# A fused attention and two MLPs on one core: the opening spread over nine slots, with five of the eight weight pairs prepared in it

## The chip, the cores and the metric

The kernel runs on one core of a Trainium2 chip. A core has a matrix engine (TensorE, PE in the rows), a vector engine (VectorE, DVE), a scalar engine (ScalarE, ACT), a general engine (GpSimd, POOL), and a sync engine (SP) whose work here is to issue transfers. Each engine takes its instructions in the order in which they were written for it; between engines semaphores decide. The metric is device time in microseconds of one execution, median over runs.

## The reference, cut to what matters

```
scores = q_c @ k_c^T / sqrt(64)          # 8 x 8 heads, 576 tokens, in chunks of 64
attn   = exp(scores - max) / (sum + 1e-9)
x      = attn @ v_c                      # -> 4608 tokens x 512
h      = relu(x @ w_in) ** 2 @ w_out     # 512 -> 2048 -> 512
out    = (silu(h @ w_gate) * (h @ w_val)) @ w_out2    # 512 -> 1536 -> 512
```

All inputs are float32 or come as float64 words (the weights), which the kernel decodes on the chip. Outputs are float32.

## The kernel before, in words

The 4608 tokens are nine blocks of 512. A block is worked as a "set": set 0 is block 0 alone, sets 1 to 4 are two blocks each, so that seven products of half size stand for eight (the class `Pair`; a single block uses `Single`). The program goes through four stages: `x @ w_in` for all sets (`up1`), then `w_out`, then gate and value, then the last product. The change touches only the first stage, and of that the part up to the end of set 1.

**Attention** comes in units of 256 tokens, two to a block. One unit's chain is: load q and k (`attn_qk`, L324); 64 small matmuls into the PSUM tile `s` (`attn_products`, L335); maximum and difference on DVE (`attn_less_max`: `mx`, `e`); exp on ACT; sum and reciprocal on DVE and a multiply on POOL (`attn_normed`, L368, into `e`); a transposition; 64 matmuls with v into `xps` (`attn_values`); four copies to `x` on ACT (`attn_out`, L450). Units 0 to 5 (`EARLY`: sets 0 and 1) are transposed on PE (`attn_turn_pe`, `et`, L392). Units of later sets are transposed by DVE into `z`, copied on ACT into `p` (L418), and then four transfers of 64 KB on SP's queue exchange quarters (`p<-z`, L422). The tiles `s` of any unit and `xps` of a later unit come from a pool with one buffer (`psa`), so they exclude each other.

**Weights** are prepared in pairs of f tiles; there are eight pairs, `("i", 0)` to `("i", 7)`. `prep_pair` (L192) is a generator of seven steps: take two raw tiles; decode on ACT (four instructions, L129 and L130); clamp and shift on DVE (L134, L135) with two adds on POOL (L139); two `m<-raw,m` instructions on DVE (L144) and two casts on ACT; the low parts and four sums on DVE (L157, L213 to L216); one cast on ACT; the last low part on DVE, and a store of the finished weights `W` (1.8 MB) for the pairs that are loaded again later. `wp` has five buffers for such `W`; pairs 0, 3 and 6 stay in three of them, the others pass through the other two.

**Products.** `up1.run(n, m)` makes the products of set n with weight pair m. A product of half size is six matmuls of 128x512. For a pair of blocks the order is px, pz, then the two late products of the run before (`p4`, `p3`) between which px is continued (`p6`), then py and px again (`p27`). Before px is continued ACT copies it away (`r1`, `u2`, `u3`, L535). For the single block a run is 24 matmuls into two `py` tiles, evicted by ACT (L603, L613), and the two late products are empty. All tiles of 4 KB per partition (q, k, v, e, z, p, raws, x, hi, lo, g) share one pool of 31 buffers (`big`); a tile waits until the last reader of its buffer is done, and for a `g` that is its store.

**The order before.** In the opening (L756) the order on PE, ACT, DVE and POOL is the written one. Slot i holds unit i's products up to its normalisation, unit i-1's transposition, unit i-2's product with v, and seven steps of preparation, three of pair i and three of pair i-1 plus one load; so eight pairs take the opening. From slot 4 on `up1.run(0, m)` follow, three in slot 4 and one in each slot after it. When the loop is over seven of the eight runs of set 0 are done, and the eighth stands behind `up1.run(1, 0)`. In the part after the opening only PE's order is the written one; the other engines' was set by a scheduler. There a run of a pair of blocks is cut into four quarters, and `WHEN` (L985) says at which quarter t of the 32 each step of the next set's four units is placed: loads at -3, 2, 6, 10, products at 2, 6, 10, 14, transposition at 6, 10, 14, 18, product with v at 11, 15, 19, 23. `OPS` (L986) places the splitting of the next set's seven operands into high and low parts.

Of the kernel before, what the change touches and what calls it, by code (L numbers as in the profile page):

```python
# [28 lines left out]
def attention_mlp_mlp_kernel(  # L29
# [29 lines left out]
    nc = tc.nc  # L59
# [9 lines left out]
    upb = BLOCK // UNIT  # L69
# [122 lines left out]
    def prep_pair(key, raws, keep, store):  # L192

        pair = raws.take(2)
        yield
        m = duo("m")
        decode1(pair, m)
        yield
        decode2(pair, m)
        yield  # L200
        decode3(pair, m)
        w = new_combo()
        a1, a22 = m[:, 0, :].rearrange("p (i c) -> p i c", i=2), m[:, 1, half:]
# [12 lines left out]
        tt(out=s4, in0=a12, in1=s2, op=ALU.subtract)  # L216
        yield
        high(s, w[:, 0, 3:7, :])
        yield
        low(s, w[:, 0, 3:7, :], w[:, 1, 3:7, :])  # L220
        if store:
            wdram[key] = combo_dram(key)
            nc.sync.dma_start(out=wdram[key], in_=flat(w))
        if keep:
            combos[key] = w
        yield
# [103 lines left out]
    def attn_v(u):  # L330
        vt = duo("v")
        loader(u).dma_start(out=vt, in_=v[2 * u:2 * u + 2].rearrange("n p c -> p n c"))
        vs[u] = vt
# [326 lines left out]
    work = Work()  # L660
# [8 lines left out]
    def raws_of(keys, ahead):  # L669
        return Raws([sources[name][2 * fp + t] for name, fp in keys for t in range(2)], ahead)  # L670
# [56 lines left out]
            self.late()  # L727


    make_identity(nc, ident)  # L730
    raws1 = raws_of(keys1, 0)
    preps = [prep_pair(key, raws1, True, key in moving1) for key in keys1]
    up1 = Products(keys1, moving1, 2, 1, lambda key: squared)

    def x_sums(n):
        up1.ops[n] = Operands()
# [1 line left out]

    early = list(range(EARLY))
    ready = {"x": upb + 2, "pair": len(early) + 2}

    def prepare(f, steps=1):
        if 0 <= f < n1:
            for _ in range(steps):
                next(preps[f])

    def loads(i):
        if i < len(early):  # L750
            attn_qk(early[i])
        prepare(i)
        if 1 <= i <= len(early):
            attn_v(early[i - 1])

    with ordered(ET.PE, ET.Activation, ET.DVE, ET.Pool):  # L756
        make_identity(nc, ident)
        loads(0)
        loads(1)
        given = 0  # L760
        for i in range(n1 + 1):
            loads(i + 2)
            unit = early[i] if i < len(early) else None
            turned = early[i - 1] if 0 <= i - 1 < len(early) else None
            valued1 = early[i - 2] if 0 <= i - 2 < len(early) else None
            if unit is not None:
                attn_products(unit)
            if turned is not None:
                attn_turn_pe(turned)
            if valued1 is not None:  # L770
                attn_values(valued1)
            prepare(i)
            prepare(i - 1)
            if i == ready["x"]:
                x_sums(0)
                up1.ops[0].make(1, 2, 4)
            prepare(i - 1)
            if i == ready["pair"]:
                x_sums(1)
                up1.ops[1].make(1, 5)  # L780
            if turned is not None:
                attn_turned(turned)
            prepare(i)
            if unit is not None:
                attn_less_max(unit)
                attn_exp(unit)
            prepare(i - 1)
            if i == ready["pair"]:
                up1.ops[1].make(6, 2, 7)
            if unit is not None:  # L790
                attn_normed(unit)
            if valued1 is not None:
                attn_out(valued1)
            if i >= ready["x"]:
                while given < min(n1, i - 1):
                    up1.run(0, given)
                    given += 1
            prepare(i)

    class Down:  # L800

# [181 lines left out]

    LAST = 4 * n1
    WHEN = {"qk": (-3, 2, 6, 10), "scores": (2, 6, 10, 14), "turn": (6, 10, 14, 18), "out": (11, 15, 19, 23)}  # L985
    OPS = {-6: (1, 5), -4: (6,), -3: (2, 7), -1: (4,)}  # L986

    def attention_step(n, t):

        if n < len(sets):  # L990
            units = [b * upb + x for b in sets[n] for x in range(upb)]
            for what in ("out", "turn", "scores", "qk"):
                for u, when in zip(units, WHEN[what]):
                    if when == t:
                        if what == "out":
                            attn_values(u)
                            attn_out(u)
                        elif what == "turn":
                            attn_v(u)
                            attn_turn(u)  # L1000
                        elif what == "scores":
                            attn_scores(u)
                        else:
                            attn_qk(u)

    def beside1(n, m):
        def at_quarter(i):
            t = 4 * m + i
            attention_step(n + 1, t)
            attention_step(n + 2, t - LAST)  # L1010
            if n + 1 < len(sets):
                if t == 24:
                    x_sums(n + 1)
                if t - LAST in OPS:
                    up1.ops[n + 1].make(*OPS[t - LAST])
            else:
                if t % 2 == 0:
                    work.step(1)
                if t == LAST - 8:
                    down1.begin()  # L1020
                if t == LAST - 4:
                    down1.split(0)

        return at_quarter

    attention_step(2, -3)
    with ordered(ET.PE):
        for n in range(1, len(sets)):
            if n + 1 == len(sets):
                raws = Raws(w_out, 2)  # L1030
                for f in range(nf1):
                    work.add(prep_plain("o", f, raws))
            for m in range(n1):
                up1.run(n, m, beside1(n, m))
                if n == 1 and m == 0:
                    up1.run(0, n1 - 1)
        up1.finish()
    combos.clear()

# [161 lines left out]
```

## Time and profile before

| | us |
|---|---|
| median of 3 runs (1661.19 to 1665.27) | 1663.77 |
| the profiled execution | 1663.95 |
| its span, first to last instruction | 1662.2 |
| PE busy in the span | 1602.5 |
| DVE busy | 1021.9 |
| ACT busy | 816.4 |

The page cuts the span into 40 slices of 41.6 us; the first three or four are the opening and set 1. A row of the timeline is an instruction, or several of one kind in a row, with its start and its length; in brackets stands how long its engine was idle before it, and what ended that. A granted clock of 1.00 is TensorE at 2.4 GHz; the other level is half of it.

### The profile page before, as it was taken

To read this page: it belongs to the slowest core of one execution; us is meant where nothing else is said; L and a number is where in the kernel's file an instruction comes from. 1 tells how busy PE (TensorE), PEld (TensorE's weight loads), DVE (VectorE), ACT (ScalarE), POOL (GpSimd) and SP (SyncE) were. 2 spreads that over 40 slices of the span, in tenths; PEclk is the share of its full clock that TensorE was granted. 3 is DMA by queue.
4 is the path that set the end of the run, shared out by engine and by line. 5 is a ranking of instruction groups with operands and counts; after the bars stand their busy time and mean duration, and the time that the engine had idled before them with its cause. 6 is when DMAs were issued, how large, how long until landed. Compare 5 with 4: busy or idle time off the path is not lost.

```text
span 1662.2 us, 23648 instructions
## 1 busy us (share of the span) xinstructions
PE 1602.5 (96%) x9408; PEld 1320.0 (79%) x9408; DVE 1021.9 (61%) x1268; ACT 816.4 (49%) x1165; POOL 156.5 (9%) x130
## 2 busy tenths in 40 slices
PE   3879999999999999999999999999999999999998
PEld 3757888888888888888888888888887787888886
DVE  7885564745377656662312645647548996877884
ACT  5775777778775444442211433434335553434441
POOL 3232121120122111110000000000000110000000
PEclk8889999999999999999999999999999999999999
DMA  8656787878876768773318686676677999663352
GB/s 326 233 222 245 256 300 287 295 275 300 317 259 222 277 243 310 283 291 128 127 38 332 255 292 212 204 267 228 216 261 284 358 402 396 233 203 122 99 147 51
DMA packets 135759, 407.10 MB, mean 245 GB/s; under 512 B 47840, under 2 KB 57056, under 8 KB 124128
## 3 DMA queue, kind: packets, MB, share of 16 engines
q1 hardware_dynamic: 115872, 347.90, 58.7%
q10 hardware_dynamic: 14592, 38.80, 6.2%
q0 software_dynamic: 5184, 18.88, 3.5%
q8 instruction: 74, 1.21, 0.3%
q14 instruction: 37, 0.30, 0.0%
HBM read 278.92 MB, written 123.47 MB: 242 GB/s over the span
## 4 chain that ended last, share of the span: by engine, by line
PE 89%; DVE 5%; DMA 3%; ACT 1%; issue 1%; POOL 0%; SPq 0%; ACTq 0%; POOLq 0%; DVEq 0%
PE px L467 11%; PE px L469 11%; PE px L468 11%; PE acc L469 6%; PE acc L468 6%; PE acc L467 6%; PE pz L469 5%; PE pz L467 5%; PE pz L468 5%; PE py L467 5%; PE py L468 5%; PE py L469 5%; PE accs L469 2%; PE accs L468 2%; PE accs L467 2%; DMA raw<-in_w_out_dram 1%
## 5 line engine op out<-in xcount | busy, mean ns | idle before, releaser
L467 PE MATMUL px<-hi,W 128*128 128x512 f32 x640 | 252.3, 394 | 9.0 <-ACT hi L154 5.4
L469 PE MATMUL px<-lo,W 128*128 128x512 f32 x640 | 250.5, 391 | 3.2 <-DVE lo L157 3.2
L468 PE MATMUL px<-hi,W 128*128 128x512 f32 x640 | 250.1, 391 | 0.0
L139 POOL TENSOR_TENSOR m<-m,raw 128x512 int32<-128x512 int32 x68 | 93.9, 1397 | 991.6 <-ACT r L535 558.9
L535 ACT COPY u<-px 128x512 f32<-128x512 f32 x160 | 92.3, 577 | 147.2 <-PE px L469 147.2
L467 PE MATMUL acc<-hi,w 128*128 128x512 f32 x416 | 161.8, 389 | 0.0
L468 PE MATMUL acc<-hi,w 128*128 128x512 f32 x416 | 161.8, 389 | 0.0
L469 PE MATMUL acc<-lo,w 128*128 128x512 f32 x416 | 161.5, 389 | 0.0
L467 PEld LDWEIGHTS px<-hi,W 128*128 128x128 f32 x640 | 120.7, 189 | 37.4 <-ACT hi L154 6.3
L469 PEld LDWEIGHTS px<-lo,W 128*128 128x128 f32 x640 | 120.7, 189 | 29.5 <-DVE lo L157 4.3
L154 ACT CAST hi<-h 128x1024 fp32r<-128x1024 f32 x93 | 95.5, 1053 | 96.6 <-DVE h L888 16.2
L157 DVE TENSOR_TENSOR lo<-graw,hi 128x1024 fp32r<-128x1024 f32 x72 | 91.4, 1270 | 83.0 <-PE acc L468 42.8
L521 DVE TENSOR_TENSOR g<-pz,u 128x512 f32<-128x512 f32 x112 | 76.8, 686 | 104.1 <-PE pz L469 61.6
L468 PEld LDWEIGHTS px<-hi,W 128*128 128x128 f32 x640 | 120.8, 189 | 24.6
L636 DVE TENSOR_TENSOR g<-g,sig 128x1024 f32<-128x1024 f32 x54 | 65.9, 1220 | 119.3 <-ACT sig L635 119.3
L467 PE MATMUL py<-hi,W 128*128 128x512 f32 x320 | 126.6, 396 | 0.3 <-DMA W<-wv 0.3
L467 PE MATMUL pz<-hi,W 128*128 128x512 f32 x320 | 125.5, 392 | 1.4 <-DVE g L521 1.3
L469 PE MATMUL pz<-lo,W 128*128 128x512 f32 x320 | 125.3, 392 | 0.4 <-DVE lo L157 0.4
L468 PE MATMUL pz<-hi,W 128*128 128x512 f32 x320 | 125.2, 391 | 0.0
L469 PE MATMUL py<-lo,W 128*128 128x512 f32 x320 | 124.7, 390 | 0.0
L468 PE MATMUL py<-hi,W 128*128 128x512 f32 x320 | 124.7, 390 | 0.0
L157 DVE TENSOR_TENSOR lo<-h,hi 128x1024 fp32r<-128x1024 f32 x93 | 110.2, 1211 | 5.4 <-ACT hi L154 2.4
(126 smaller groups left out, 3134.3 us busy)
## 6 DMA issues: line engine op xcount, KB each, us to landing
W<-wv SPq DMA_DIRECT2D x30, 1792.0 KB, 8.8
g<-g ACTq DMA_DIRECT2D x72, 512.0 KB, 5.3
graw<-g SPq DMA_DIRECT2D x72, 512.0 KB, 4.2
W<-wi SPq DMA_DIRECT2D x20, 1792.0 KB, 9.9
W<-wg SPq DMA_DIRECT2D x20, 1792.0 KB, 8.4
h<-g SPq DMA_DIRECT2D x54, 512.0 KB, 8.3
h<-h SPq DMA_DIRECT2D x54, 512.0 KB, 6.3
raw<-in_w_out_dram SPq DMA_DIRECT2D x28, 512.0 KB, 7.8
```

Of the source, the lines that this page charges most:

```text
L139: nc.gpsimd.tensor_tensor(out=mi[:, t, :], in0=mi[:, t, :], in1=word(raw, 0, I32), op=ALU.add)
L154: nc.scalar.copy(out=hi, in_=src)
L157: nc.vector.tensor_tensor(out=lo, in0=src, in1=hi, op=ALU.subtract)
L467: nc.tensor.matmul(out=ps, lhsT=lh, rhs=rh, start=first, stop=False, skip_group_check=on)
L468: nc.tensor.matmul(out=ps, lhsT=ll, rhs=rh, start=False, stop=False, skip_group_check=on)
L469: nc.tensor.matmul(out=ps, lhsT=lh, rhs=rl, start=False, stop=last, skip_group_check=on)
L521: nc.vector.tensor_tensor(out=o, in0=ps, in1=r, op=ALU.add)
L535: nc.scalar.copy(out=r, in_=self.x)
L636: nc.vector.tensor_tensor(out=g[j], in0=g[j], in1=s, op=ALU.mult)
```

## The change

The opening becomes nine slots. A unit's chain takes one slot more: transposition two slots after its products, product with v three slots after them. Each slot takes four steps of preparation from one queue of all pairs (37 steps with the one ahead of the loop, so five pairs and two steps of the sixth), not seven. Set 0's runs 0 to 3 stand one each in slots 5 to 8. Runs 4 to 7 of set 0 stand behind runs 1, 2, 3 and 5 of set 1 (`between`), and the remaining three pairs are prepared beside set 1, a step to a quarter. Set 1 uses the weights as they were prepared and loads none again (`since` is 2, not 1). Set 2's four units move later and closer: `WHEN1`. Everything from set 2's products on is the same.

```diff
-    raws1 = raws_of(keys1, 0)
-    preps = [prep_pair(key, raws1, True, key in moving1) for key in keys1]
-    up1 = Products(keys1, moving1, 2, 1, lambda key: squared)
+    raws1 = raws_of(keys1, 2)
+    for key in keys1:
+        work.add(prep_pair(key, raws1, True, key in moving1))
+    up1 = Products(keys1, moving1, 2, 2, lambda key: squared)
...
-    ready = {"x": upb + 2, "pair": len(early) + 2}
...
+    ready = upb + 3
+    between = {1: 4, 2: 5, 3: 6, 5: 7}
...
         loads(0)
+        work.step()
         loads(1)
-        given = 0
-        for i in range(n1 + 1):
+        for i in range(len(early) + 3):
             loads(i + 2)
-            unit = early[i] if i < len(early) else None
-            turned = early[i - 1] if 0 <= i - 1 < len(early) else None
-            valued1 = early[i - 2] if 0 <= i - 2 < len(early) else None
+            unit, turned, valued1 = (early[i - d] if 0 <= i - d < len(early) else None for d in (0, 2, 3))
...
-            prepare(i)
-            prepare(i - 1)
-            if i == ready["x"]:
+            work.step()
+            if i == ready:
                 x_sums(0)
                 up1.ops[0].make(1, 2, 4)
-            prepare(i - 1)
-            if i == ready["pair"]:
-                x_sums(1)
-                up1.ops[1].make(1, 5)
             if turned is not None:
                 attn_turned(turned)
-            prepare(i)
             if unit is not None:
                 attn_less_max(unit)
+            work.step()
+            if unit is not None:
                 attn_exp(unit)
-            prepare(i - 1)
-            if i == ready["pair"]:
-                up1.ops[1].make(6, 2, 7)
+            if valued1 is not None:
+                attn_out(valued1)
+            work.step()
             if unit is not None:
                 attn_normed(unit)
-            if valued1 is not None:
-                attn_out(valued1)
-            if i >= ready["x"]:
-                while given < min(n1, i - 1):
-                    up1.run(0, given)
-                    given += 1
-            prepare(i)
+            work.step()
+            if i >= ready:
+                up1.run(0, i - ready)
+        x_sums(1)
+        up1.ops[1].make(1, 5)
+        up1.ops[1].make(6, 2, 7)
...
+    WHEN1 = {"qk": (9, 12, 15, 18), "scores": (12, 15, 18, 21), "turn": (15, 18, 21, 24), "out": (17, 20, 23, 26)}
...
+    OPS1 = {-4: (1, 5), -3: (6,), -2: (2, 7), -1: (4,)}
...
-                for u, when in zip(units, WHEN[what]):
+                for u, when in zip(units, (WHEN1 if n == 2 else WHEN)[what]):
...
+            if n == 1:
+                work.step()
...
-                if t == 24:
+                if t == (24 if n > 1 else 27):
                     x_sums(n + 1)
...
-                if n == 1 and m == 0:
-                    up1.run(0, n1 - 1)
+                if n == 1 and m in between:
+                    up1.run(0, between[m], lambda i: work.step())
```

PE, beside set 1, where unit 6's product with v stands. Before (`px_1712` and `px_1874` are products of set 1, with hi and lo parts of its operands):

```order
L469 MATMUL px_1712<-lo_1413,W_1632 128x512
L467 MATMUL px_1712<-hi_1412,W_1632 128x512
L468 MATMUL px_1712<-hi_1412,W_1632 128x512
L469 MATMUL px_1712<-lo_1413,W_1632 128x512
L442 MATMUL xps_1833<-p_1636,v_1634 64x64 x32
L467 MATMUL px_1874<-hi_1393,W_708 128x512
```

And in the changed kernel (`px_1818`, `py_1939`: products of the same run of set 1, its fifth):

```order
L469 MATMUL px_1818<-lo_1267,W_1128 128x512
L467 MATMUL px_1818<-hi_1266,W_1128 128x512
L468 MATMUL px_1818<-hi_1266,W_1128 128x512
L469 MATMUL px_1818<-lo_1267,W_1128 128x512
L442 MATMUL xps_1842<-p_1710,v_1708 64x64 x32
L343 MATMUL s_1891<-k_1763,q_1762 64x64 x32
L467 MATMUL py_1939<-hi_1270,W_1128 128x512
```

Unit 8's products (`s_1891`) now stand directly behind unit 6's `xps`; before there were products of set 1 between such two.

SP's queue, beside set 1. Before (`wi` are the prepared weights in memory, `W` a load of them, `p<-z` a unit's exchange):

```order
L223 DMA wi7_1402<-W_1375 128x3584
L422 DMA p_1636<-z_1637 32x512 x2
L230 DMA W_1632<-wi2_694 128x3584
L422 DMA p_1636<-z_1637 32x512 x2
L230 DMA W_1755<-wi4_1103 128x3584
L422 DMA p_1759<-z_1760 32x512 x4
L422 DMA p_1921<-z_1922 32x512 x2
L230 DMA W_1917<-wi5_1242 128x3584
L422 DMA p_1921<-z_1922 32x512 x2
L422 DMA p_2075<-z_2076 32x512 x4
L230 DMA W_2185<-wi7_1402 128x3584
```

And in the changed kernel:

```order
L223 DMA wi5_1374<-W_1313 128x3584
L422 DMA p_1710<-z_1711 32x512 x4
L422 DMA p_1883<-z_1884 32x512 x4
L422 DMA p_2031<-z_2032 32x512 x4
L223 DMA wi7_1598<-W_1552 128x3584
L230 DMA W_2184<-wi1_553 128x3584
L422 DMA p_2222<-z_2223 32x512 x4
L230 DMA W_2436<-wi2_727 128x3584
```

The loads of `W` for set 1 are gone from between the exchanges; the last unit's exchange (`p_2222`) stands behind the store of pair 7 and the load of pair 1 for set 2.

ACT, from the copy of unit 6's `p` on. Before (`g_1456`, `g_1457`: outputs of run 0 of set 1; `g_1548`: run 7 of set 0; `r_1616`, `u_1630`: the first two copies of px of run 1 of set 1; `e` is unit 7's exp):

```order
L418 COPY p<-z 128x1024
L614 DMA g_0_112<-g_1456 128x1024
L612 ACTIVATE g_1457<-g_1457 128x1024
L613 ACTIVATE g_1457<-g_1457 128x1024
L603 ACTIVATE g_1548<-py 128x512
L614 DMA g_0_120<-g_1457 128x1024
L613 ACTIVATE g_1548<-g_1548 128x1024
L535 COPY r_1616<-px 128x512
L614 DMA g_7_111<-g_1548 128x1024
L535 COPY u_1630<-px 128x512
L366 ACTIVATE e<-e 128x1024
```

And in the changed kernel (`g_1616`, `g_1617`: outputs of run 3 of set 1; `g_1766`: run 6 of set 0; `r_1826`: the first copy of px of run 4 of set 1):

```order
L418 COPY p<-z 128x1024
L366 ACTIVATE e<-e 128x1024
L603 ACTIVATE g_1766<-py 128x512
L603 ACTIVATE g_1616<-px 128x512
L613 ACTIVATE g_1616<-g_1616 128x1024
L614 DMA g_3_115<-g_1616 128x1024
L612 ACTIVATE g_1617<-g_1617 128x1024
L613 ACTIVATE g_1617<-g_1617 128x1024
L603 ACTIVATE g_1766<-py 128x512
L614 DMA g_3_123<-g_1617 128x1024
L613 ACTIVATE g_1766<-g_1766 128x1024
L535 COPY r_1826<-px 128x512
```

The exp of unit 7 now stands directly behind the copy of unit 6's `p`, ahead of seven evictions and of `r_1826`; before it stood behind the evictions and the copies of px.

## Rows read from the trace of the kernel before

**Rows 1.** The page: busy time by engine, and PE in 40 slices.
```profile
PE 1602.5 (96%) x9408; PEld 1320.0 (79%) x9408; DVE 1021.9 (61%) x1268; ACT 816.4 (49%) x1165; POOL 156.5 (9%) x130
...
PE   3879999999999999999999999999999999999998
```

**Rows 2.** Busy us by stretch (PE, PEld, DVE, ACT, POOL); granted clock, DMA share, GB/s.
```profile
21.49:33.43 11.94, 5.33 (x134) 5.03 (x132) 11.77 (x17) 7.50 (x13) 4.67 (x3) 0.64 1.04 397
...
57.42:81.40 23.98, 23.98 (x352) 20.37 (x349) 16.65 (x22) 18.17 (x29) 4.73 (x3) 0.97 0.41 153
...
93.52:118.03 24.51, 20.68 (x218) 16.97 (x214) 16.70 (x25) 17.41 (x32) 9.04 (x7) 0.92 0.56 208
...
162.00:226.68 64.68, 64.68 (x622) 52.45 (x612) 33.78 (x40) 48.41 (x75) 7.40 (x7) 1.00 0.77 274
```

**Rows 3.** Timeline of PE: set 1's first products, and set 3's first unit.
```profile
118.03 0.80 PE L467 MATMUL px<-hi,W 128*128 128x512 f32 x1 [3.83 <-ACT hi L154]
...
122.41 0.63 PE L467 MATMUL px<-hi,W 128*128 128x512 f32 x1
122.83 0.63 PE L468 MATMUL px<-hi,W 128*128 128x512 f32 x1
...
226.68 1.16 PE L343 MATMUL s<-k,q 64*64 64x64 f32 x64
```

**Rows 4.** Timeline of PE: set 0's runs 0 to 2, third and last matmul.
```profile
60.11 0.44 PE L469 MATMUL py<-lo,W 128*128 128x512 f32 x1
...
75.83 0.39 PE L469 MATMUL py<-lo,W 128*128 128x512 f32 x1
```

**Rows 5.** Timeline of DVE: a slot's attention part, then set 1's sums.
```profile
22.82 1.22 DVE L361 TENSOR_REDUCE mx<-s 128x16 f32<-128x1024 f32 x1
...
25.21 1.43 DVE L157 TENSOR_TENSOR W<-s,W 128x1024 fp32r<-128x1024 f32 x1
26.57 1.21 DVE L371 TENSOR_REDUCE sums<-e 128x16 f32<-128x1024 f32 x1
...
28.18 2.93 DVE L144 SCALAR_TENSOR_TENSOR m<-raw,m 128x512 int32<-128x512 int32 x2
...
115.87 1.22 DVE L505 TENSOR_TENSOR t<-x,x 128x1024 f32<-128x1024 f32 x1
...
125.08 2.35 DVE L157 TENSOR_TENSOR lo<-x,hi 128x1024 fp32r<-128x1024 f32 x2
```

**Rows 6.** Timeline of ACT: eviction of a run of set 0, a decode, a cast.
```profile
87.38 1.13 ACT L603 ACTIVATE g<-py 128x512 f32<-128x512 f32 x2
88.55 1.06 ACT L613 ACTIVATE g<-g 128x1024 f32<-128x1024 f32 x1
...
91.55 0.67 ACT L129 ACTIVATE m<-raw 128x512 f32<-128x512 f32 x1
...
93.81 1.03 ACT L154 CAST W<-s 128x1024 fp32r<-128x1024 f32 x1
```

**Rows 7.** Timelines of PE, DVE and SP: a later unit, from its products to its exchange.
```profile
238.03 1.16 PE L343 MATMUL s<-k,q 64*64 64x64 f32 x64
...
247.14 1.25 DVE L414 STREAM_TRANSPOSE z<-e 128x1024 f32<-128x1024 f32 x1 [2.09 <-POOL e L375]
...
249.49 2.64 SPq L422 DMA_DIRECT2D p<-z  x4
```

**Rows 8.** The tile p: exchanges issued at 249.5 behind a W, at 239.1, at 186.1.
```profile
DMA to landing us min/median/max: 13.1/13.2/13.3
...
DMA to landing us min/median/max: 6.9/7.1/7.2
...
DMA to landing us min/median/max: 2.0/2.4/3.3
```

**Rows 9.** Timeline of ACT: the copies of a later unit's xps.
```profile
254.57 1.18 ACT L458 COPY x<-xps 128x256 f32<-128x256 f32 x4
```

**Rows 10.** The page's DMA issues: KB each, median us to landing.
```profile
g<-g ACTq DMA_DIRECT2D x72, 512.0 KB, 5.3
```

More of the change, by code (lines that the diff above doesn't have):

```diff
@@ L727, in finish @@
             self.late()
-    make_identity(nc, ident)
-    raws1 = raws_of(keys1, 0)
-    preps = [prep_pair(key, raws1, True, key in moving1) for key in keys1]
-    up1 = Products(keys1, moving1, 2, 1, lambda key: squared)
+    raws1 = raws_of(keys1, 2)
+    for key in keys1:
+        work.add(prep_pair(key, raws1, True, key in moving1))
+    up1 = Products(keys1, moving1, 2, 2, lambda key: squared)
     def x_sums(n):
@@ L741, in attention_mlp_mlp_kernel @@
     early = list(range(EARLY))
-    ready = {"x": upb + 2, "pair": len(early) + 2}
[L744 to L747, printed above, removed]
+    ready = upb + 3
+    between = {1: 4, 2: 5, 3: 6, 5: 7}
     def loads(i):
@@ L751, in loads @@
             attn_qk(early[i])
-        prepare(i)
-        if 1 <= i <= len(early):
-            attn_v(early[i - 1])
+        if 2 <= i < len(early) + 2:
+            attn_v(early[i - 2])
     with ordered(ET.PE, ET.Activation, ET.DVE, ET.Pool):
@@ L771, in attention_mlp_mlp_kernel @@
                 attn_values(valued1)
-            prepare(i)
-            prepare(i - 1)
-            if i == ready["x"]:
+            work.step()
+            if i == ready:
                 x_sums(0)
                 up1.ops[0].make(1, 2, 4)
-            prepare(i - 1)
-            if i == ready["pair"]:
-                x_sums(1)
-                up1.ops[1].make(1, 5)
             if turned is not None:
                 attn_turned(turned)
-            prepare(i)
             if unit is not None:
                 attn_less_max(unit)
+            work.step()
+            if unit is not None:
                 attn_exp(unit)
-            prepare(i - 1)
-            if i == ready["pair"]:
-                up1.ops[1].make(6, 2, 7)
+            if valued1 is not None:
+                attn_out(valued1)
+            work.step()
             if unit is not None:
                 attn_normed(unit)
-            if valued1 is not None:
-                attn_out(valued1)
-            if i >= ready["x"]:
-                while given < min(n1, i - 1):
-                    up1.run(0, given)
-                    given += 1
-            prepare(i)
+            work.step()
[4 more added lines that the diff above has]
+        up1.ops[1].make(6, 2, 7)
     class Down:
@@ L1011, in at_quarter @@
             if n + 1 < len(sets):
-                if t == 24:
+                ops = OPS if n > 1 else OPS1
+                if t == (24 if n > 1 else 27):
                     x_sums(n + 1)
-                if t - LAST in OPS:
-                    up1.ops[n + 1].make(*OPS[t - LAST])
+                if t - LAST in ops:
+                    up1.ops[n + 1].make(*ops[t - LAST])
             else:
@@ L1024, in beside1 @@
         return at_quarter
-    attention_step(2, -3)
     with ordered(ET.PE):
```

## The prediction

> **What bounds the kernel now.** I read the page first: PE is busy for 96% of the span, and only the first slices of the 40 stand below 9 [rows 1]. So time is to be had in the opening and in set 1 alone, and from there on the program is one stream of matmuls. Next I cut the opening by slot. In slot 1 DVE is busy for 11.77 of 11.94 us and PE for 5.33, at a granted clock of 0.64 [rows 2]: early slots are as long as their DVE work. In the stretches 57.42 to 81.40 and 93.52 to 118.03 DVE idles for 7.3 and 7.8 us, while ACT waits for the runs of set 0 that PE works on [rows 2]. From 162.00 PE never idles [rows 2]. That gives two marks. Set 1's first product starts at 118.03, and unit 10's `s` (set 3's first) starts at 226.68 [rows 3]; from that instruction on PE's order is the same in both kernels, so the change is worth what it moves this second mark.
>
> **What lies between the marks.** The order of instructions has 378 matmuls of 128x512 there and eight groups of 64 small ones (`s`, `xps`). Matmul 3 and matmul 72 of set 0's runs start 15.72 us apart [rows 4]: 69 steps of 0.228 us at full clock. An `s` takes 1.16 [rows 3]. So 378 x 0.228 + 8 x 1.16 = 95.5 us of work in 108.65; 13.2 us are lost before, all of it ahead of 162.00.
>
> The changed kernel has 72 matmuls more between its own marks (runs 4, 5 and 6 of set 0 move behind the start of set 1): 450 x 0.228 + 9.3 = 111.9 us. If set 1 starts at A and L is lost after that, the second mark is A + 111.9 + L.
>
> **A, the opening.** A unit's part on DVE is 22.82 to 25.21 and 26.57 to 28.18, 4.0 us [rows 5]; the rest of slot 1, 7.9 us, is one weight pair. Three of eight pairs leave: 3 x 7.9 = 23.8 us less DVE work ahead of set 1's first sum, which stood at 115.87 [rows 5]. Against it stand waits. Before, the two stretches held 15.1 us of them. After, I take 17.6: with fewer steps in a slot, DVE has less beside POOL's add of each pair, and in slots 6 to 8 the cast that DVE needs stands on ACT behind a run's evictions (1.13 + 1.06 [rows 6]) and a decode of 2.26 (91.55 to 93.81 [rows 6]). First sum: 115.9 - 23.8 + 2.5 = 94.6. The early products with a cold PE hide behind DVE as they did. That a unit's transposition comes a slot later takes PE's wait for POOL out of the slot, but PE had room there, so I count nothing; were DVE not the longer one, it would be some us of the 11.94.
>
> Set 1's first high part then waits for ACT, which has by its written order a decode (2.3), one raw of the next pair (0.6), the evictions of run 3 (2.2), a store's issue (0.4) and the cast itself (1.0): 6.4 us. A = 101.0, 17.0 earlier. Bounds: no wait but POOL's adds would give some 12 us less, hence 91 with ACT's queue; a full slot's wait at each of the four runs (5.5 us, 24 x 0.228, for 3 of them more than before) 111. I take 101, near the sum of rows.
>
> **L, what is lost in set 1.** The sum has four terms.
>
> 1. Operands. From the first sum to the last low part DVE took 115.87 to 127.43, 11.6 us [rows 5]. Now pair 5's steps stand between (two L144, 2.9 [rows 5], and a clamp): 4 more, so the last low part is ready at 94.6 + 15.6 = 110.2, where PE would be at 101 + 24 x 0.228 = 106.5. That is 3.7, and 1.3 for six or seven matmuls at the lower clock, 0.42 apart and not 0.23 [rows 3], as PE had it at the same place before. 5.0.
>
> 2. Copies of px. Behind an inserted run of set 0 the late products of the run before are gone, so only six matmuls (1.4 us) lie between px and its continuation, and ACT must copy px in that time. At three places ACT is at most one pass late (1.06 [rows 6]); I take 1 in all. At the fourth it is worse, because ACT's order there has two waits. From the start of unit 6's `s` its `z` is ready after 10.4 (238.03 to 247.14 + 1.25 [rows 7]); unit 7's maximum and difference stand behind it on DVE (2.4 [rows 5]), its exp behind that (1.1), and then seven evictions (6.5) and the copy (0.6): 21.0. PE reaches the continuation after 67 matmuls and two units' `s`, 17.6. 3.4 lost; 4.4 together. Were DVE to take unit 7's maximum earlier, this falls to 1.
>
> 3. Unit 8's `s` stands directly behind unit 6's `xps` in the one-buffer pool. It waits for the four copies (1.18 [rows 9]) and two hand-overs: 1.6. Nothing can hide it on PE; behind it every matmul is queued.
>
> 4. Exchanges. From a unit's `s` to the last of its four exchange issues pass 238.03 to 252.1, 14 us; landing takes 2.4 to 7.1 after that where the queue is free [rows 7, 8]. Before, `xps` followed some nine quarters after `s`; now five. Unit 6: covered by the wait of term 2. Unit 7: `z` needs a buffer that the stores of run 6's `g` still hold (5.3 to landing [rows 10], issued behind the late copy of term 2), so its exchange lands 33 to 38 us after unit 6's `s`, and PE is there after 33: I take 2. Unit 8: 16 to 21 against 17.8: 2.5. Unit 9: its exchange stands on SP behind a load of W that can only start when pair 5's buffer is released, 30 matmuls (6.8 us) ahead of `xps`. An exchange behind a W landed 13.2 after its issue [rows 8]; the W is issued at once, the exchange a little later, and I take 11.3 from the release: 4.5. Together 9.0; all hidden 0, each at its worst 18. What is saved on this queue, five loads of W of 1.8 MB for set 1, frees transfers while none of these four waits hangs on them, so it counts nothing; what such a load cost PE before is in the 13.2.
>
> The Trainium skill (DMA: Bandwidth & Descriptors, Queues, rings and completion order) says that what SP issues runs through one ring on each DMA engine and is consumed in ring order; the trace agrees, 13.2 us behind a W and 2.4 alone. By the fit of the same page (Anatomy of one DMA: 2.0 us and bytes over 436 GB/s) W and exchange would be an estimate of 6 to 7 us, nothing of the 4.5 would be left, and the time would be 1666; the rows are of this kernel and decide.
>
> Sum: L = 5.0 + 4.4 + 1.6 + 9.0 = 20.0. Second mark: 101.0 + 111.9 + 20.0 = 232.9, against 226.68: 6.2 us later. The profiled execution is 1663.95 (span 1662.2), 0.2 over the median of 1663.77, so 1663.95 + 6.2 = 1670. L of 13.8 would be no change.
>
> **Rivals.**
>
> *Faster: the later part hides its waits.* The place is set 1 from unit 6 on. DVE gets unit 7's maximum early, exchanges land 2.4 after issue as at 186.1 [rows 8], unit 9's W finds the engines free: L = 5 + 1 + 1.6 + 1 = 8.6, and ACT's decode lies in a wait of PE, so A is 98.7. 98.7 + 111.9 + 8.6 = 219.2, 7.5 us less: 1656.5. For it: DMA had 0.77 of its share in 162 to 226.68 [rows 2] and loses five loads of W. Against it: the order of SP and ACT is fixed, and PE has no spare work. It decides from L under 9. The Trainium skill (Perfetto Trace Analysis, Optimization Strategy) says that interleaving stretches with different limits can improve a kernel, which is what the change does with weight preparation and products; the rows of the opening agree that the limits differ (DVE 11.77, PE 5.33 in one slot), but not that the receiving stretch has room in its chains.
>
> *No change.* Half of term 4 and the milder case of term 2: L = 14 to 15, 1664.
>
> *The opening doesn't get shorter as it should.* The round through PE's run, its eviction, the decode behind it and the cast bounds slots 5 to 8 at a full eviction more each, A = 108: 1677. For it: PE idled 3.83 us for a cast of ACT before [rows 3]. Against it: DVE loses 23.8 us of work in any case.
>
> **How the numbers follow.** Forecast (1670, own range 1665 to 1676): 0.45. Faster: 0.22. No change: 0.20. Longer opening: 0.13. Differences under 0.3%, 5 us, count as none, about what can be told here. Faster by more: most of the first rival and the edge of others, 0.19. Within: the third case, the forecast's low edge and the first rival's high one, 0.31. Slower: 0.50. The range leaves out one in ten on either side: 1656 to 1679, from the first rival's time to a little over the last.
>
> **What would show it.** Right: set 1's first product near 101 with a wait for ACT's high part; unit 9's `xps` late by 3 to 6 us for a DMA; unit 8's `s` late by 1.6 for ACT; px of run 4 late for the copy `r`; set 3's first `s` near 233. Wrong: PE without waits from unit 6 on, or set 1's first product at 108 or at 92; also any shift behind the second mark, where I expect the same time to the end.

## The result, and the profile after

The changed kernel takes 1672.4 us in the median of four runs (1670.8 to 1673.1), the kernel before 1663.9 (1661.2 to 1665.3): a ratio of 1.0054, 95% interval 1.0042 to 1.0066, slower by some 8.5 us. The profiled execution took 1672.67 with a span of 1670.8, 8.6 over that of before.

The page of after, to be held against [rows 1]: PE's busy time has risen by 3 us, DVE's and ACT's hardly at all. The work is the same, and only the first slices tell of a difference.

```profile
PE 1605.6 (96%) x9408; PEld 1321.4 (79%) x9408; DVE 1024.5 (61%) x1268; ACT 815.7 (49%) x1165; POOL 158.1 (9%) x128
...
PE   3689899999999999999999999999999999999998
```

Busy time by stretch in after (PE, PEld, DVE, ACT, POOL; granted clock, DMA share, GB/s), to be held against [rows 2]. The second row is the start of set 1, the third and fourth lie on either side of the longest wait.

```profile
57.42:81.40 23.98, 17.56 (x271) 14.49 (x269) 19.74 (x22) 16.55 (x29) 7.46 (x4) 0.91 0.52 188
...
100.00:108.00 8.00, 3.63 (x8) 2.32 (x8) 8.00 (x7) 5.89 (x8) 4.39 (x2) 0.68 0.43 180
200.00:212.02 12.02, 7.21 (x31) 5.35 (x30) 0.89 (x2) 6.05 (x8) 0.00 (x0) 1.00 0.98 361
212.02:236.12 24.10, 23.44 (x149) 19.11 (x149) 14.76 (x15) 15.92 (x24) 2.89 (x4) 0.86 0.43 149
```

PE had no idle time in the first of these stretches before [rows 2]; now it is idle for 6.4 us there. At set 1's start DVE is busy for all 8 us, and PE waits for ACT's first cast (the row of 103.23 below). From 200 the transfers are busy for 0.98 of their time, and after the wait that ends at 212.02 the clock is at 0.86: part of what follows runs at the lower of its two levels.

The timeline of PE in after (start, length, idle before and what ended it). The rows at 103.23 and 236.12 are the two marks, 118.03 and 226.68 in [rows 3].

```profile
75.20 0.52 PE L467 MATMUL py<-hi,W 128*128 128x512 f32 x1 [4.32 <-ACT g L603]
...
103.23 0.79 PE L467 MATMUL px<-hi,W 128*128 128x512 f32 x1 [5.29 <-ACT hi L154]
...
170.69 0.50 PE L467 MATMUL px<-hi,W 128*128 128x512 f32 x1 [3.01 <-ACT r L535]
...
176.29 1.16 PE L343 MATMUL s<-k,q 64*64 64x64 f32 x64 [1.33 <-ACT x L458]
...
187.87 1.16 PE L343 MATMUL s<-k,q 64*64 64x64 f32 x64 [0.69 <-ACT x L458]
...
212.02 0.47 PE L442 MATMUL xps<-p,v 64*64 64x64 f32 x4 [4.79 <-DMA p<-z]
213.15 1.97 PE L442 MATMUL xps<-p,v 64*64 64x64 f32 x60 [0.66 <-DMA p<-z]
...
236.12 1.16 PE L343 MATMUL s<-k,q 64*64 64x64 f32 x64
```

So set 1 starts 14.8 us earlier, and set 3's first `s` 9.4 us later. Between the marks lie 132.89 us with 111.9 of work; 21.0 are lost, where 13.2 were lost before. The 60 small matmuls at 213.15 take 1.97 us, the 64 of other rows 1.16: that is the lower clock after the wait. From the second mark to the end both spans agree: 1670.8 - 236.12 = 1434.7 and 1662.2 - 226.68 = 1435.5.

Below, A is the start of set 1's first product, M that of set 3's first `s`, and L = M - A less the work between them.

| kernel | time, us | ratio, 95% | A | M | L |
|---|---|---|---|---|---|
| before, measured beside each group | 1662.7 to 1663.9 | | 118.03 | 226.68 | 13.2 |
| after | 1672.4 | 1.0042 to 1.0066 | 103.23 | 236.12 | 21.0 |
| e1: one W load on another queue | 1672.2 | 1.0045 to 1.0073 | 103.10 | 236.12 | 21.1 |
| e2: two steps fewer in the opening | 1673.8 | 1.0049 to 1.0074 | 101.05 | 237.61 | 24.7 |
| e3: new opening, old groups | 1688.0 | 1.0136 to 1.0163 | 104.45 | 251.69 | 35.3 |
| e4: old opening, new groups | 1677.2 | 1.0069 to 1.0097 | 117.06 | 240.47 | 27.9 |
| e5: W load written behind | 1672.7 | 1.0044 to 1.0069 | 102.81 | 235.51 | 20.8 |
| e6: units 8 and 9 earlier | 1672.7 | 1.0040 to 1.0067 | 102.75 | 235.20 | 20.5 |
| e7: all pairs in the opening | 1679.1 | 1.0081 to 1.0108 | 145.04 | 242.17 | 7.1 |
| e8: spread alone | 1664.6 | 1.0003 to 1.0021 | 121.03 | 229.85 | 13.3 |
| e9: units spaced by four | 1665.1 | 1.0001 to 1.0018 | 103.07 | 227.78 | 12.8 |
| e10: 29 buffers | 1695.7 | 1.0177 to 1.0205 | 103.89 | 251.04 | 35.2 |
| e11: spaced by four, last one late | 1668.4 | 1.0024 to 1.0052 | 103.15 | 232.89 | 17.8 |
| e12: spaced by four, one group later | 1668.9 | 1.0026 to 1.0051 | 103.20 | 233.01 | 17.9 |

The work is 95.5 us where the opening is the old one (before, e4, e8), 90.0 in e7, which has one run of set 0 fewer (24 x 0.228) between the marks, and 111.9 elsewhere. A, M and L are of one profiled execution each.

### The profile page after: what moved, and what is told of

Its sections match the earlier page's. It is cut to its first block, busy times and chain, and to the rows that moved or that the text cites. A ratio compares the mean times of both kernels' runs of the same rounds, so it can differ in the third digit from the quotient of the medians.

```text
span 1670.8 us, 23654 instructions
## 1 busy us (share of the span) xinstructions
PE 1605.6 (96%) x9408; PEld 1321.4 (79%) x9408; DVE 1024.5 (61%) x1268; ACT 815.7 (49%) x1165; POOL 158.1 (9%) x128
## 4 chain that ended last, share of the span: by engine, by line
PE 88%; DVE 5%; DMA 2%; issue 2%; ACT 2%; POOL 0%; SPq 0%; ACTq 0%; POOLq 0%; DVEq 0%
PE px L467 11%; PE px L469 11%; PE px L468 11%; PE acc L469 6%; PE acc L468 6%; PE acc L467 6%; PE pz L469 5%; PE pz L467 5%; PE pz L468 5%; PE py L467 5%; PE py L468 5%; PE py L469 5%; PE accs L469 2%; PE accs L468 2%; PE accs L467 2%
```

## The experiments

**Which half of the change costs: e3 and e4.** The change has two parts that can be had apart: the opening with three pairs moved beside set 1, and the later, closer groups of set 2's units. e3 is after with the old groups:

```diff
-    for u, when in zip(units, (WHEN1 if n == 2 else WHEN)[what]):
+    for u, when in zip(units, WHEN[what]):
...
+    attention_step(2, -3)
```

> The changed kernel with its new opening and its new distribution of preparation, but with the units of attention of set 2 at the groups of set 1 where the kernel before has them (the first unit's scores back in the opening). Theory (the later and closer units cost the time: px behind r 3.0 us at 170.69, scores behind the transposed products' eviction 1.3 us at 176.29 and 0.7 at 187.87, the last unit's exchange 5.5 us and the low clock after it): these 10 to 13 us go, the second mark (set 3's first scores) falls from 236.12 to 223 to 228 us with the scores of one unit added to the opening, and the time is 1660 to 1664 us, at or below the kernel before. Rival (the three pairs prepared beside set 1's blocks hold up its evictions and operands, whenever the units run): the mark stays at 233 us or later and the time at 1669 to 1673 us.

(What stands in the opening again is only the loads of the first unit's q and k.) The theory fell: 1688.0 us, 15.5 over after. PE and DVE of e3, from their timelines:

```profile
153.48 0.79 PE L467 MATMUL pz<-hi,W 128*128 128x512 f32 x1 [9.18 <-DVE g L521]
```

```profile
129.61 1.23 DVE L157 TENSOR_TENSOR lo<-x,hi 128x1024 fp32r<-128x1024 f32 x1 [6.12 <-DMA g<-g]
146.95 0.69 DVE L521 TENSOR_TENSOR g<-py,r 128x512 f32<-128x512 f32 x1 [3.08 <-DMA p<-z]
152.73 0.69 DVE L521 TENSOR_TENSOR g<-pz,u 128x512 f32<-128x512 f32 x1 [5.09 <-DMA g<-g]
188.08 1.25 DVE L414 STREAM_TRANSPOSE z<-e 128x1024 f32<-128x1024 f32 x1 [4.98 <-DMA g<-g]
```

DVE waits here for transfers of tiles that it doesn't read: a `g`, a `lo` or a `z` gets a buffer of the common pool only when a store or an exchange has let go of it. So the 31 buffers, which raws, decoded pairs and the units' tiles share, do not last there.

e4 is before with `WHEN1` and `OPS1` for set 2, and nothing else.

> The kernel before, with its own opening and all pairs prepared there, but with the units of set 2 at the changed kernel's groups of set 1 (none in the opening). Theory (the later units cost by themselves): from the first product of set 1 (about 118 us, or up to 2 us earlier without the unit's scores in the opening) to set 3's first scores it takes 113 to 119 us against 108.65 before, and the time is 1667 to 1673 us. Rival (later units cost only where preparation runs beside them): 108 to 111 us for the stretch, and a time of 1662 to 1666 us.

1677.2 us, somewhat over the theory's range; its M - A is 123.4. PE of e4:

```profile
178.54 0.50 PE L467 MATMUL px<-hi,W 128*128 128x512 f32 x1 [2.11 <-ACT r L535]
183.48 2.37 PE L442 MATMUL xps<-p,v 64*64 64x64 f32 x64 [2.54 <-DMA p<-z]
```

No preparation runs here beside set 1, and still units stand too close to their exchanges. So the late groups cost 13.8 us by themselves (1677.2 against 1663.4 beside it); with the new opening the old groups cost 24.5 and the new ones 8.5. The two parts can't be added up.

**What holds unit 9's exchange: e1 and e5.** e1 issues the load of `W_2184` on POOL's queue (`queue = nc.gpsimd if early_load.pop(key, None) else nc.sync`, with `early_load` naming that one load).

> The changed kernel with one load moved: the reload of the first W of set 2 (1.8 MB) is issued on GpSimd's queue instead of SyncE's, where in the changed kernel it stands right ahead of unit 9's four 64 KB exchanges (load issued at 200.15 us, exchanges at 201.45 to 203.6, landing 9.4 to 9.9 us after issue). Theory (the exchanges wait behind the load on their own queue): the exchanges land 2 to 7 us after issue, TensorE's wait for them at 212.02 (4.79 us, and 0.66 after it) falls to 0 to 2 us, the clock stays up through 216 to 236 us (0.93 there now), and the run comes out 5 to 8 us below the changed kernel, 1664 to 1667 us. Rival (the 64 KB exchanges share the 16 DMA engines with the load whatever queue it is on, at 317 GB/s in 200 to 216 us): landing stays at 8 to 10 us, the wait at 4 to 6 us, and the time within 1 us of 1672.4.

The rival came true. PE and the tile p (196 to 216 us) of e1:

```profile
211.35 0.33 PE L445 MATMUL xps<-p,v 64*64 64x64 f32 x4 [4.14 <-DMA p<-z]
```

```profile
DMA to landing us min/median/max: 7.6/9.0/9.6
```

In after it was 9.4 to 9.9. How the load and the exchange shared the engines can be read from the queues in 204 to 208 us (packets, MB, share; the load is on q1, SP's, in after and on q0 in e1). First after, then e1:

```profile
q1 hardware_dynamic: 72, 1.03, 62.1%
...
q0 software_dynamic: 136, 1.28, 77.7%
q1 hardware_dynamic: 45, 0.07, 4.5%
```

In after 72 packets for 1.03 MB are 14 KB each, as the load's rows; the exchange's rows have 2 KB, so none of it has moved yet. In e1 the exchange moves beside the load, but in small packets: 0.07 MB against 1.28. The wait in the queue is gone, and slow progress has taken its place. e5 writes the load behind the exchanges in the program (a helper issues it at the end of `attn_turn` of unit 9).

> The changed kernel with the reload of set 2's first W (1.8 MB) issued on SyncE right behind unit 9's four exchanges instead of right ahead of them. Moving the load to another queue left the exchanges' landing at 9.0 us (from 9.5) and TensorE's wait at 4.14 and 1.26 us. Theory (all that is in flight shares the DMA engines, 400 to 440 GB/s in 200 to 208 us, and 1.8 MB ahead of or beside the exchanges costs some 4 us): with the load behind them they land in 3 to 6 us, the wait falls to 0 to 2 us, the clock stays up, and the time is 1664 to 1668 us. Rival (the stores of g and the loads of v ahead of them are enough, or the eviction at 200.39 us is simply too late): landing 7 us or more, wait 3 us or more, time 1670 to 1673 us.

This one tells nothing apart: SP's order is not the written one there, and the load still went first. SP of e5:

```profile
199.65 0.33 SPq L240 DMA_DIRECT2D W<-wi  x1
200.96 2.75 SPq L431 DMA_DIRECT2D p<-z  x4
```

The order was the other one in e9 and e12, below, where the units' places differ too.

**The first product of set 1: e2.** The last slot's last two preparation steps are left to set 1 (at both places of the loop):

```diff
-            work.step()
+            if i < len(early) + 2:
+                work.step()
```

> The changed kernel with the last two preparation steps of the opening's last slot left out, so that the sixth pair's decode begins only in set 1 and ScalarE has no decode (96.76, 98.44 us) ahead of the cast of set 1's first operand (102.13 us). Theory (the first product of set 1 stands at 103.23 us because ScalarE and VectorE serve the sixth pair first): it starts 2 to 3 us earlier, at 100.2 to 101.2, and if set 1's preparation has room for the two steps the time falls by as much, to 1669.4 to 1670.4 us. Rival (the start is set by the length of the chain from the last x through sums and operands, not by what is queued ahead): it moves by less than 1 us and the time stays within 0.5 us of 1672.4; if the two steps push a later pair's W past its products, it is 1 to 3 us slower.

A is 2.2 us earlier, as the theory had it, and the time is not shorter: 1673.8 against 1672.4, their intervals overlap. PE of e2:

```profile
101.05 0.79 PE L467 MATMUL px<-hi,W 128*128 128x512 f32 x1 [4.18 <-ACT hi L154]
...
170.25 0.79 PE L467 MATMUL px<-hi,W 128*128 128x512 f32 x1 [3.02 <-ACT r L535]
```

At the wait for `r` it is 0.4 us ahead of after (170.69), and by unit 9's `xps` 1.5 behind. An earlier start of PE alone brings nothing. Whether that is because the chains on the other engines don't start earlier, or because of the two steps that set 1 has to do in addition, e2 doesn't tell apart.

**Moving two units alone: e6.** `scores` (12, 15, 16, 19), `turn` (15, 18, 20, 22), `qk` (9, 12, 13, 16), outputs as in after.

> The changed kernel with units 8 and 9 of set 2 earlier by two groups in scores (groups 16 and 19 in place of 18 and 21) and in the turn (20 and 22 in place of 21 and 24), their outputs where they were. No scores stand right behind another unit's xps any more, and unit 9's exchange is issued ahead of the fourth run of set 0. Theory (the changed kernel pays 1.3, 0.8 and 0.7 us for scores behind xps, and some 9 us for unit 9's late exchange with the low clock behind it): 8 to 11 us go, second mark at 225 to 229 us, time 1661 to 1665 us. Rival (a new wait takes their place: exponentials and copies of units 8 and 9 now fall among the evictions of the third run of set 0, as px waited 3.0 us at 170.69 for those of units 6 and 7): the mark at 231 us or later, time 1667 us or more.

The rival again: unit 9's `xps` no longer waits, and the time is the same. PE of e6, then DVE:

```profile
173.04 0.76 PE L467 MATMUL px<-hi,W 128*128 128x512 f32 x1 [4.77 <-ACT r L535]
...
190.79 2.10 PE L442 MATMUL xps<-p,v 64*64 64x64 f32 x64 [4.42 <-issue]
```

```profile
187.61 0.69 DVE L521 TENSOR_TENSOR g<-pz,u 128x512 f32<-128x512 f32 x1 [6.37 <-DMA p<-z]
```

DVE stands for 6.37 us before a `g` until an exchange has let go of a buffer. The `mx` and `e` that read the `s` of 180.88 stand behind that on DVE and end at 190.68; `xps`, which shares the one-buffer pool with `s`, starts at 190.79. What was saved at one place (9 us) is paid at two others.

**The spread by itself: e7 and e8.** e7 draws after's opening out to fourteen slots, with all pairs in it.

```diff
-        for i in range(len(early) + 3):
+        for i in range(n1 + ready):
-    between = {1: 4, 2: 5, 3: 6, 5: 7}
+    between = {}
```

(and the old groups, old `OPS`, `since` 1.)

> The changed kernel's opening with the chain of each unit over two slots, but drawn out to fourteen slots, so that all eight pairs are prepared and all of set 0 runs in it, as in the kernel before; set 1, its units' groups and its W's reloads are those of the kernel before. What is left of the change is the spread of the chain. Theory (the spread by itself brings little, since the opening is bound by the preparation of the pairs, four steps a slot, and by the operands at its end): set 1's first product at 117 to 122 us (118.03 before), the time 1662 to 1668 us. Rival (the spread takes the opening's waits away, TensorE's 4 to 5 us for the normed units at 42.6, 54.6 and 90.7 us, and so the start is earlier by their sum): start at 105 to 111 us and time 1651 to 1658 us.

Neither: the start is at 145.04. PE and ACT of e7:

```profile
134.06 0.79 PE L467 MATMUL py<-hi,W 128*128 128x512 f32 x1 [9.37 <-ACT W L154]
```

```profile
125.35 1.06 ACT L613 ACTIVATE g<-g 128x1024 f32<-128x1024 f32 x1
...
126.86 0.66 ACT L129 ACTIVATE m<-raw 128x512 f32<-128x512 f32 x1 [0.46 <-ACT g L613]
...
133.38 1.01 ACT L154 CAST W<-m 128x512 fp32r<-128x512 f32 x2 [4.21 <-DVE m L144]
```

With one queue of steps a pair begins only when the one before is done, and its decode stands on ACT behind the eviction of a run that PE could not start without the pair before. That closes a ring: 17.3 us from one run to the next (116.75 to 134.06) with 5.5 us of matmuls in it. e8 is before with only the spread (transposition two slots after the products, values three, one slot more), pairs prepared two at a time as before.

> The kernel before with only the spread of each unit's chain over two slots (its transposes two slots after its scores, its values three), one slot more (ten for nine) and set 0's runs one slot later; pairs are prepared as in the kernel before, two at a time, and all but the last run of set 0 stands in the opening. From set 1 on TensorE's order is that of the kernel before. Theory (the spread takes away TensorE's waits for the normed units, 4.06, 4.0 and 4.93 us, but the preparation of the pairs and the extra slot hold the opening's length): set 1's first product at 114 to 119 us (118.03 before) and the time 1659 to 1665 us. Rival 1 (the waits go and nothing takes their place): start at 106 to 110 us, time 1651 to 1656 us. Rival 2 (the extra slot costs a slot, about 10 us): start at 122 to 128 us, time 1667 to 1674 us.

1664.6 us, a ratio of 1.0003 to 1.0021: the theory's result. Its profiled execution has A at 121.03, 2 us past the range, and was itself 2 us over the median. Rivals 1 and 2 are out.

**Buffers: e10.** After with `bufs=29` for the pool of 31.

> The changed kernel with 29 buffers instead of 31 in the large pool that raw weights, decoded pairs, q, k, v, e, z, p, x and g share. In the changed kernel VectorE stands 6.76 us before z of unit 7 (173.03 us) because that z takes the buffer of a g whose store has not landed. Theory (set 1 beside which pairs are prepared is held by buffers): with two less the waits of VectorE for a store or an exchange in 103 to 236 us rise from 7.8 us to 12 us or more, and the mark from 236.1 to 239 to 246 us, time 1675 to 1682 us. Rival (buffers hold VectorE where TensorE doesn't wait for it): the waits move, the mark stays within 2 us of 236.1 and the time within 2 us of 1672.4.

The time is far beyond the theory (1695.7, 23 over after), and its sign of it is wrong: DVE's waits for transfers in the stretch did not rise (6.4 us for 7.8; its longest wait, 7.09 us before a `z`, is one for which the trace names no cause). PE of e10:

```profile
160.03 1.16 PE L343 MATMUL s<-k,q 64*64 64x64 f32 x64 [2.62 <-DMA k<-in_k_dram]
...
206.16 0.48 PE L442 MATMUL xps<-p,v 64*64 64x64 f32 x4 [5.76 <-DMA p<-z]
```

The shortage shows as loads of k and exchanges that come late, 15 us up to M, and more behind it (M is 14.9 later, the span 22.7). That the stretch is near the edge of its buffers is shown; that each single wait of after is due to them is not.

**Spacing: e9, e11, e12.** e9 is after with one line changed:

```diff
-    WHEN1 = {"qk": (9, 12, 15, 18), "scores": (12, 15, 18, 21), "turn": (15, 18, 21, 24), "out": (17, 20, 23, 26)}
+    WHEN1 = {"qk": (3, 7, 11, 15), "scores": (7, 11, 15, 19), "turn": (11, 15, 19, 23), "out": (14, 18, 22, 26)}
```

> The changed kernel with set 2's units spaced by four groups instead of three and earlier (scores at groups 7, 11, 15, 19; turns at 11, 15, 19, 23; outputs at 14, 18, 22, 26). Theory (what set 1 loses comes of units standing close together late: the late groups alone cost the kernel before 14 us): unit 9's exchange is issued earlier, no wait at its xps, second mark at 224 to 231 us, time 1660 to 1667 us. Rival (units that run beside the preparation of the last three pairs wait with it for ACT, DVE and buffers, as with the old groups, where set 1 took 147 us and g waited 9.2 us for a buffer): mark at 236 us or later, time 1672 to 1682 us.

1665.1 us: 7.3 of the 8.5 us are back, M is 8.3 earlier than in after. PE, SP and the tile p (196 to 216 us) of e9:

```profile
140.13 0.80 PE L467 MATMUL px<-hi,W 128*128 128x512 f32 x1 [4.06 <-ACT r L535]
```

```profile
199.35 3.68 SPq L422 DMA_DIRECT2D p<-z  x4
203.14 0.51 SPq L230 DMA_DIRECT2D W<-wi  x1
```

```profile
DMA to landing us min/median/max: 3.0/3.2/3.6
```

Unit 9's exchange is now issued 3.8 us ahead of the load and lands in 3 us. e11 keeps the spacing of four but unit 9 as late as in after (scores 9, 13, 17, 21; outputs 16, 20, 23, 26).

> The changed kernel with set 2's units spaced by four groups (scores at 9, 13, 17, 21) but with unit 9 as late as there: scores 21, turn 24, output 26, so that its exchange is issued at the same place of the order. (Units spaced by four and ended a group or two earlier gave 1665.1 us, mark 227.78.) If closeness is what costs: px waits for r and scores behind xps go, unit 9's xps waits 0 to 2 us, mark 226 to 230 us, time 1663 to 1668 us. If the lateness of the last unit costs: r and scores as before the spacing go (some 5 us), but xps of unit 9 still waits 4 to 5 us with the low clock behind it, mark 230 to 234 us, time 1667 to 1671 us.

M at 232.89 and 1668.4 us: the second reading. SP and p of e11, load first again:

```profile
198.26 0.33 SPq L230 DMA_DIRECT2D W<-wi  x1
199.56 2.73 SPq L422 DMA_DIRECT2D p<-z  x4
```

```profile
DMA to landing us min/median/max: 8.5/8.7/9.0
```

So of the 8.3 us between after and e9 the spacing, which also puts units 6 to 8 earlier, gives 3.2 (236.12 to 232.89) and the earlier end 5.1. e12 is e9 one group later, but for the turn of unit 9 and the outputs of units 8 and 9 (scores 8, 12, 16, 20; turns 12, 16, 20, 23; outputs 15, 19, 22, 26).

> The changed kernel with set 2's units spaced by four groups, scores at 8, 12, 16, 20, turns at 12, 16, 20, 23, outputs at 15, 19, 22, 26: one group later than the version that gave 1665.1 us, where px waited 4.06 us at 140.13 for r, whose copy stood on ScalarE behind unit 6's exponential and the sixth pair's casts of W. Theory (with the exponential a group later, behind r): that wait falls to 2 to 3 us, the others stay, mark 226 to 227.5 us, time 1663 to 1665 us, not beyond the bound of no change. Rival (closer to the changed kernel's late units, waits at xps or scores come back): mark 229 to 233 us, time 1667 to 1671 us.

The wait for `r` went, as the theory had it; the rival's waits came (PE of e12):

```profile
160.38 0.33 PE L442 MATMUL xps<-p,v 64*64 64x64 f32 x4 [2.30 <-DMA p<-z]
...
184.40 1.72 PE L442 MATMUL xps<-p,v 64*64 64x64 f32 x60 [1.90 <-DMA p<-z]
```

Unit 9's exchange, ahead of the load there too, landed in 4.2 to 4.9 us. Still M is 5.2 later than in e9, as late as in e11: the gain of e9 is not that of the exchange alone, and one group's shift is enough to lose it. No version beat the kernel before.

## Why the prediction came out right, point by point

The forecast was 1670.0 and M at 232.9; measured were 1672.4 and 236.12. Of the 3.2 us of difference in M, 2.2 came in A and 1.0 in L.

*A: 101.0 forecast, 103.23 measured.* Set 1's first sum was forecast for 94.6 and stood at 96.99 (DVE of after); from there to the first product it took 6.2 us where I had 6.4.

```profile
96.99 1.22 DVE L505 TENSOR_TENSOR t<-x,x 128x1024 f32<-128x1024 f32 x1
```

The term that was wrong is DVE's work, which I let decide. Busy time up to the first sum (PE, PEld, DVE, ACT, POOL), before and after:

```profile
0.00:115.87 115.87, 75.76 (x1320) 66.24 (x1320) 89.10 (x121) 76.83 (x131) 38.30 (x33) 0.88 0.68 258
...
0.00:96.99 96.99, 58.67 (x1245) 52.06 (x1246) 70.94 (x90) 59.67 (x104) 27.29 (x22) 0.88 0.61 229
```

18.2 us of DVE's work left, not 23.8. My price of 7.9 a pair came from slot 1, where a pair's two L144 took 2.93 us [rows 5]; in the last slots they took 2.38. One step of the last pair stood behind the sum already before, and some of what stayed grew: L500 took 1.22 us before and 2.92 in after. The waits came out smaller than I had them: DVE was idle for 26.8 us up to the sum before and for 26.1 in after, where I had 2.5 more. The two errors, 5.6 and 3.2 us, point opposite ways; that A came within 2.2 is in part luck.

For the total the work of PE counts too. PE had been busy for all of 57.42 to 81.40 [rows 2]; what leaves the opening on PE is three runs, 16.4 us, and the opening became 14.8 shorter. So the move gives 1.6 us away before any wait of set 1. e9, where L is nearly what it was before, fits that: M is 1.1 later, the time 0.1% longer.

*Term 1, operands: 5.0 forecast, 4.0 measured* (time of PE over its work at 103 to 110 us; DVE busy throughout). The split was the other way round: 3.7 of wait and 1.3 of lower clock forecast, 1.1 of wait measured, and the rest matmuls 0.42 apart, at a granted clock of 0.52.

*Term 2, copies of px: 4.4 forecast, 3.2 measured*, at run 4 alone, by the queue on ACT that I had followed, and 1.2 more for the five matmuls behind it at the lower clock; the places where I took 1 us in all cost nothing.

*Term 3, unit 8's `s`: 1.6 forecast, 2.0 measured*, 1.33 of it wait, the rest the slow `xps` ahead of it (1.73 us for 1.16). The same neighbourship of unit 9's `s` and unit 7's `xps` (0.69 of wait, 0.8 in all) I overlooked.

*Term 4, exchanges: 9.0 forecast, 8.6 measured*, but not where I had put them. Units 7 and 8 (2 and 2.5 forecast) waited for nothing. Unit 9 cost all of it: 5.45 of wait (4.5 forecast), and some 3.1 of lower clock behind, which I had not counted (212.02 to 236.12 are 24.1 us, with 20.3 of work and 0.66 of that wait). That the sum is nearly right is luck: two waits that did not come stand against a cost that I had left out. DVE of after shows why a buffer matters at unit 7, as forecast:

```profile
173.03 1.25 DVE L414 STREAM_TRANSPOSE z<-e 128x1024 f32<-128x1024 f32 x1 [6.76 <-DMA g<-g]
```

SP of after, and p in 195 to 216 us, answer to [rows 8]: the load goes first, and the exchange lands in 9.5 us, between 2.4 alone and 13.2 behind a W.

```profile
200.15 0.33 SPq L230 DMA_DIRECT2D W<-wi  x1
201.45 2.76 SPq L422 DMA_DIRECT2D p<-z  x4
```

```profile
DMA to landing us min/median/max: 9.4/9.5/9.9
```

The order within the ring, which the prediction named, holds: in 204 to 208 us of after nothing of the exchange had moved, only the load. The kernel before has both cases in one unit, two transfers issued ahead of a load and two behind it:

```profile
142.78 1.26 SPq L422 DMA_DIRECT2D p<-z  x2
144.71 0.32 SPq L230 DMA_DIRECT2D W<-wi  x1
145.07 1.16 SPq L422 DMA_DIRECT2D p<-z  x2
```

```profile
DMA to landing us min/median/max: 2.9/6.8/10.1
```

The two ahead landed in 2.9 to 3.7 us, the two behind in 9.9 to 10.1. What the runs add is that another queue would not have helped: there the same load held the exchange nearly as long (e1: 9.0 us), while issued behind the exchange it did not (e9: 3.2, e12: 4.7). The engines that all queues draw on were busy for 0.98 of 200 to 212 us.

The Trainium skill (DMA: Bandwidth & Descriptors, Queues, rings and completion order) has, beside the order within a ring that the prediction named, a rule on arbitration: an engine takes turns between the queues that have work, a packet from each. The trace of e1 is in line with it, 45 packets of SP's queue while the load moved on the other; what the rule calls a packet need not be what the profile counts as one. That so small a share is why the exchange gained only 0.5 us is a reading that no run tests. By the fit of the same page of the Trainium skill (Anatomy of one DMA), that the prediction named, nothing of the wait would have been left (an estimate). It stands there for GpSimd's path and for each transfer by itself; here the load on GpSimd's queue took 12.0 us to land in e1, so the trace does not bear it out for engines as busy as these.

*The rivals.* "The later part hides its waits" failed at its condition, L under 9; none of the kernels with three pairs beside set 1 came below 12.8. "No change" is what e9 gives, by better placed units, not by milder waits of this change. "The opening doesn't get shorter" was met by less than a third: A was past my value by 2.2 of the 7 us in question, and DVE's waits up to the first sum did not grow as a whole.

What I had right for a reason that the runs bear out: the receiving stretch has no slack in its chains as the units stand. e6 shows it best, one cost of some 9 us removed and nearly as much returned elsewhere; e2, where 2.2 us were brought to set 1 and given back, agrees, though set 1 had two steps more to do there. The places of the units decide how much that costs: e9, with one line changed, has 7.3 of the 8.5 us back.

## What to carry to other kernels

Before work is moved out of an opening, reckon what each engine gives up there and what each must do later: DVE's work fell by 18.2 us and the opening by 14.8, while 16.4 us of PE's matmuls had to be done later, so the move lost before any wait. A stretch that receives work is judged by its chains and its free buffers, not by its engines' busy shares; change the places of all units together and measure each, since moving two units alone (e6), or all by one group (e12), brought up other waits. And a small transfer that something waits for should be issued ahead of a large one, on whatever queue; putting the large one on another queue did not help.

## What the runs showed of the hardware that was not expected

Four exchanges of 64 KB took 9.4 to 9.9 us with a load of 1.8 MB issued 1.3 us ahead on the same queue, 7.6 to 9.6 with it 1.2 us ahead on another, 3.0 to 3.6 with it behind. On the other queue its packets moved beside the load's, on the same queue none of them had moved while the load did (204 to 208 us). And a wait of 5 us cost TensorE more than itself: after that of 212.02 the granted clock over the next 24 us was 0.86, some 3.1 us more.
